# Hash attention and a gated feed-forward: the first batch's preparation rearranged across ScalarE, VectorE, GpSimd and the DMA queues

## The chip, the cores and the metric

The kernel runs on one core of one Trainium2 chip. The metric is the device time of the program in microseconds. A core has TensorE (PE in the profile, with its weight loads as PEld), VectorE (DVE), ScalarE (ACT), GpSimd (POOL) and SyncE (SP, which here only issues DMAs).

## The reference

For 4 batches and 8 heads of 768 tokens by 64, attention is masked by a hash: a query sees the keys that lie in the same of 64 buckets. The result is laid out token by token and goes through an RMS norm and a gated feed-forward.

```python
q_bits = (np.einsum('bhsd,dk->bhsk', q, proj) > 0)          # 6 bits; the same for k
q_bucket = np.sum(q_bits * powers, axis=-1)
mask = q_bucket[:, :, :, None] == k_bucket[:, :, None, :]
scores = np.where(mask, scale * np.matmul(q, k.transpose(0, 1, 3, 2)), -1e9)
attn = softmax(scores)                                       # with + 1e-09 in the divisor
attn_out = np.matmul(attn, v)
x = attn_out.transpose(0, 2, 1, 3).reshape(3072, 512)
xn = x / sqrt(mean(x * x) + 1e-06) * rms_g
out = (silu(xn @ w_gate) * (xn @ w_val)) @ w_out             # 512 -> 1536 -> 512
```

## The kernel before, in words

**The order.** Nothing is scheduled by a planner. Each step is put on one list with a position (`at(pos, fn)`), the list is sorted by position at the end, and the program is issued in that order. Each engine works through its own steps in that order, and so do the DMA queues of SP and of POOL. Position n is the place of slot n; negative positions are the start.

**Units and slots.** A unit is half a batch's queries (384 of 768) for all 8 heads; there are 8 units. A unit has 24 slots: slot n is head n // 3 and a third of its keys. `scores` (L344) makes two matmuls of 71 rows by 384 queries, and ACT takes the exponential of each (L351) into `p`. `pv(n)` follows some slots later: six matmuls that add p times v (L375), and once per pair of heads one with `vsum` (L363). `post` (L391, L392) divides by the sum on DVE. `pvpool` has one buffer, so the next pair's first pv waits for it.

**The 71 rows.** The mask is in the product. A tile `qk` holds 64 rows of q or k, six rows of bits (+0.5 or -0.5) and a constant row; a score whose bits differ falls far below the others, and the exponential drops it. So before a slot can run, its pair of heads must be prepared:
- `tr_mm` (L202): three fp32 transposes of a loaded block on PE; `tr_ev`: its copy to qT or kT by ACT (L209) or DVE (L211). Steps j = 0 and 2 are q of the two heads, 1 and 3 are k.
- the hash: matmuls with the projection. Pairs A and B (batch 0, first two) use `hash_head` per head (L245), C and D (the other two) and later pairs `hash_mm` for the whole pair (L216). Four matmuls stand side by side in four column groups of PE.
- the bits: either `direct_head` or `direct` (L252, L222), in which DVE writes six rows straight into qk, or `bits` (L229), in which DVE writes all groups to a tile and `place` (L235) carries each group of six rows to qk by a DMA of SP.
- `dims_head`, `dims`: the 64 rows of qT or kT cast to fp16 into qk, by POOL (L266, L276), DVE (L264, L274) or ACT (L262). In `dims(c, e)` c = 0 is q, 1 is k, and e is the half (first or second 384 tokens). Unit 0 needs the first half of q and both halves of k; q's second half (0, 1) is for unit 1.
- `vcast` (L280 on DVE and POOL) and `vsum` (L288 to L291, three adds on POOL): v in fp16 and its sums.

**Around them.** PSUM has `ring` (4 buffers: scores, transposes, pair hashes, transposed x), `gvpool` (3: head hashes, some of unit 0's scores, later the gates) and `pvpool`. Loads of q and k (L71, L72) and of v (L78) are issued by SP into four stage buffers each. Weights are loaded by POOL's queue: `load_gv` (L174) gate and value, `load_wo` (L178).

**After a unit.** `queue_norm`: `rstd` (a power on POOL, L443), three `xn` on DVE (L450), transposes on PE (L463), copies to xnT. `queue_gates`: 12 steps, each eight matmuls (L502), a tanh on ACT (L511), two DVE products (L519, L528). For unit 0 the norm stands at position 24.6, its transposes at 30.8, its gates from 32 on, between unit 1's slots; the output matmuls (L566) follow in the next unit. Batch 1's first two pairs are prepared at positions 17.3 (pair (1,0)) and 24.56 (pair (1,1)), with DVE copies in part, and their `dims` at positions 32.2 to 41.5.

Of the kernel before, what the change touches and what calls it, by code (L numbers as in the profile page):

```python
# [22 lines left out]
HQ = 384  # L23
# [10 lines left out]
def kernel(  # L34
# [12 lines left out]
    nc = tc.nc  # L47
# [4 lines left out]
    work = ctx.enter_context(tc.tile_pool(name="work", bufs=2))  # L52
    ring = ctx.enter_context(tc.tile_pool(name="ring", bufs=4, space=PSUM))
# [6 lines left out]
    def at(pos, fn):  # L60
        queue.append((pos, len(queue), fn))
# [5 lines left out]
    def load_qk(b, hp):  # L67
        ql = stage.tile([128, 2, 6, D], FP32, name="ql", tag="ql")
        kl = stage.tile([128, 2, 6, D], FP32, name="kl", tag="kl")
        hs = slice(2 * hp, 2 * hp + 2)  # L70
        nc.sync.dma_start(out=ql, in_=q[b, hs].rearrange("h (p c) d -> p h c d", c=6))  # L71
        nc.sync.dma_start(out=kl, in_=k[b, hs].rearrange("h (p c) d -> p h c d", c=6))  # L72
        loads[(b, hp)] = [ql, kl]

    def load_v(b, hp):
        vl = stage.tile([128, 2, 6, D], FP32, name="vl", tag="vl")
        hs = slice(2 * hp, 2 * hp + 2)
        nc.sync.dma_start(out=vl, in_=v[b, hs].rearrange("h (p c) d -> p h c d", c=6))  # L78
        vloads[(b, hp)] = vl
# [44 lines left out]
    pj1 = []  # L124
# [55 lines left out]

    prep_n = [0]
    qk_of = {}

    def make_prep(b, hp):

# [4 lines left out]
        tl = {}  # L190
# [45 lines left out]
                out=qk[64:70, c, HQ * e : HQ * e + HQ], in_=tl["bits"][base : base + 6, :]  # L236
            )

        GROUPS = [(0, 0), (1, 0), (1, 1), (0, 1)]

        def hash_head(h):
            m = gvpool.tile([128, HQ], FP32, name="hps", tag="gv")
            tl["h", h] = m
            for g, (c, e) in enumerate(GROUPS):
                nc.tensor.matmul(  # L245
# [4 lines left out]
        def direct_head(h, g):  # L250
            c, e = GROUPS[g]
            nc.vector.tensor_scalar(  # L252
                qk[64:70, 2 * c + h, HQ * e : HQ * e + HQ],
                tl["h", h][32 * g : 32 * g + 6, :],
                0.0, 0.5, op0=ALU.is_gt, op1=ALU.subtract,
            )
# [28 lines left out]
        def vsum():  # L285
# [325 lines left out]
    A(-20.5, "tr_mm", 2)  # L611
    A(-20.5, "tr_ev", 2, "a")
    A(-20.4, "tr_mm", 3)
    A(-20.4, "tr_ev", 3, "v")
    A(-20.3, "direct_head", 0, 2)
    at(-20.2, lambda: keep_warm(2))

# [6 lines left out]
    Bp(1.05, "tr_mm", 0)  # L624
    Bp(1.06, "tr_ev", 0, "a")
    Bp(1.1, "tr_mm", 1)
    Bp(1.1, "tr_ev", 1, "v")
    A(1.2, "direct_head", 0, 3)
    A(1.3, "vcast")
    Bp(1.4, "dims_head", 0, 0, 0, "p")  # L630
    Bp(1.4, "dims_head", 0, 1, 0, "p")
# [3 lines left out]
        Bp(2.05, "direct_head", 0, g)  # L635
    Bp(2.1, "tr_mm", 2)
    Bp(2.1, "tr_ev", 2, "a")
    Bp(3.05, "tr_mm", 3)
    Bp(3.05, "tr_ev", 3, "v")
    A(3.1, "direct_head", 1, 3)  # L640
    Bp(3.2, "dims_head", 1, 0, 0, "p")
    Bp(3.2, "dims_head", 1, 1, 0, "p")
    Bp(3.2, "dims_head", 1, 1, 1, "p")
    A(3.3, "vsum")
    Bp(4.05, "hash_head", 1)
    for g in range(3):
        Bp(4.05, "direct_head", 1, g)
    Bp(4.1, "direct_head", 0, 3)
    Bp(4.1, "direct_head", 1, 3)
    Bp(4.5, "vcast")  # L650
    Bp(4.6, "vsum")
    for j in range(4):
        C((4.9, 5.4, 6.0, 6.6)[j], "tr_mm", j)
        C((4.9, 5.4, 6.0, 6.6)[j], "tr_ev", j)
    C(7.6, "hash_mm")
    C(7.6, "direct", 0)
    C(7.6, "direct", 2)
    C(7.6, "bits")
    for i, (c, e) in enumerate(PLACES[2:]):
        C((7.61 if e == 0 or c > 1 else 12.0) + 0.01 * i, "place", c, e)  # L660
    for i, (c, e) in enumerate([(0, 0), (1, 0), (1, 1)]):
        C(7.9 + 0.1 * i, "dims", c, e, "ppv"[i])
    C(8.3, "vcast", nc.vector)
    C(8.5, "vsum")
    for j in range(4):
        Dp(8.1 + 0.8 * j, "tr_mm", j)
        Dp(8.1 + 0.8 * j, "tr_ev", j)
    Dp(11.4, "hash_mm")
    Dp(11.4, "bits")
    for i, (c, e) in enumerate(PLACES):  # L670
        Dp((11.41 if e == 0 or c > 1 else 12.2) + 0.01 * i, "place", c, e)
    for i, (c, e) in enumerate([(0, 0), (1, 0), (1, 1)]):
        Dp(13.7 + 0.3 * i, "dims", c, e, "v")
    Dp(14.8, "vcast", nc.vector)
    Dp(11.5, "vsum")
    for i, P in enumerate((A, Bp, C, Dp)):
        P((15.0, 19.0, 28.5, 31.5)[i], "dims", 0, 1)


    for c in range(4):  # L680
        for wh in range(2):
            at((7.0, 11.8, 14.0, 16.0)[c] + 0.1 * wh, lambda c=c, wh=wh: load_gv(c, wh))
# [52 lines left out]
    for u in range(NU):  # L735
        base = SLOTS * (u + 1)
# [40 lines left out]
```

## Time and profile before

| | us |
|---|---|
| median of 3 runs (lowest, highest) | 365.52 (365.12, 365.79) |
| the profiled execution, whole | 363.95 |
| its span on the core | 362.2 |
| PE, DVE, ACT, POOL busy in the span | 346.8, 243.3, 239.0, 69.1 |
| mean granted clock of PE | 0.994 |

The span runs from the first instruction to the last; the execution's time has 1.75 us around it. Times in the views are us from the span's start, durations of groups are us in total unless a mean in ns is named. PE's busy time includes time in which a started matmul waits for its operand, so a busy PE is not always a PE at its peak. The page cuts the span into 40 slices of 9.05 us; PE's busy tenths are 8976979899 in the first ten and 9 in nearly all others.

### The profile page before, as it was taken

How to read it: one execution, taken by the hardware profiler on the slowest of the kernel's cores; microseconds unless marked ns; L12 is line 12 of the kernel's file. 1: busy time of each engine (PE TensorE's matmuls, PEld its weight loads, DVE VectorE, ACT ScalarE, POOL GpSimd, SP SyncE). 2: the span in 40 equal slices, each digit the busy share in tenths (PEclk: the TensorE clock that was granted, in tenths of full speed). 3: DMA queues.
4: the chain of work that ended last, by engine and by line, in shares of the span. 5: the costliest groups of instructions: out<-in, count | busy, mean ns of one | idle time of the engine just before them, and what ended most of it. 6: DMA issues, size and time to landing. Idle time of an engine off the chain costs nothing.

```text
span 362.2 us, 8037 instructions
## 1 busy us (share of the span) xinstructions
PE 346.8 (96%) x3081; PEld 213.9 (59%) x3081; DVE 243.3 (67%) x494; ACT 239.0 (66%) x544; POOL 69.1 (19%) x108
## 2 busy tenths in 40 slices
PE   8976979899999999999999999999999999999996
PEld 4544645566656656666656666666566656665653
DVE  5887797957855684767757586666847565476771
ACT  3666677676767777776767766776767766873421
POOL 3699172500000003242000001424000000000000
PEclk9999899999999999999999999999999999999999
DMA  7998987300005505220003703420001100200202
GB/s 245 374 265 126 249 151 169 43 3 2 4 3 173 179 3 179 89 90 2 4 3 93 261 2 121 147 93 1 5 3 53 40 2 0 90 2 1 89 0 87
DMA packets 24030, 31.20 MB, mean 86 GB/s; under 512 B 2084, under 2 KB 20920, under 8 KB 23992
## 3 DMA queue, kind: packets, MB, share of 16 engines
q1 hardware_dynamic: 17768, 25.64, 21.0%
q0 software_dynamic: 5824, 4.72, 8.9%
q8 instruction: 24, 0.39, 0.4%
q10 hardware_dynamic: 400, 0.34, 0.3%
q14 instruction: 14, 0.11, 0.1%
HBM read 28.58 MB, written 6.29 MB: 96 GB/s over the span
## 4 chain that ended last, share of the span: by engine, by line
PE 85%; DVE 12%; issue 1%; ACT 1%; POOL 0%; DVEq 0%
PE v_ps L502 17%; PE o_ps L566 16%; PE g_ps L502 16%; PE s_ps L344 15%; PE pv L375 8%; PE trps L202 5%; DVE qk L274 4%; PE hps L216 3%; DVE xn L450 2%; PE xtp L463 1%; PE pv L363 1%; PE hps L245 1%; PE wps L107 1%; DVE a L519 1%; DVE sq L405 1%; DVE bits L229 1%
## 5 line engine op out<-in xcount | busy, mean ns | idle before, releaser
L351 ACT ACTIVATE p<-s_ps 128x384 f16<-128x384 f32 x384 | 163.3, 493 | 62.6 <-PE s_ps L344 62.3
L344 PE MATMUL s_ps<-qk 71*128 71x384 f16 x384 | 95.3, 328 | 5.4 <-DVE qT L211 1.9
L502 PE MATMUL v_ps<-xnT,wv 128*128 128x384 f16 x384 | 78.1, 326 | 2.4 <-DVE a L519 2.4
L519 DVE SCALAR_TENSOR_TENSOR a<-th,g_ps 128x384 f32<-128x384 f32 x96 | 53.1, 553 | 38.7 <-ACT th L511 37.3
L502 PE MATMUL g_ps<-xnT,wg 128*128 128x384 f16 x384 | 78.4, 325 | 0.3 <-ACT xnT L471 0.2
L375 PEld LDWEIGHTS <-p 128*128 128x128 f16 x1152 | 59.8, 98 | 24.9 <-issue 2.5
L566 PE MATMUL o_ps<-wo,ht 128*128 128x512 f16 (+1 forms) x300 | 68.7, 370 | 0.0
L375 PE MATMUL pv<-v,p 128*128 128x65 f16 x1152 | 66.7, 194 | 1.0 <-DVE x L392 0.7
L511 ACT ACTIVATE th<-g_ps 128x384 f32<-128x384 f32 x96 | 47.9, 499 | 17.4 <-PE g_ps L502 15.4
L528 DVE TENSOR_TENSOR ht<-a,v_ps 128x384 f16<-128x384 f32 x96 | 53.1, 553 | 9.2 <-PE s_ps L344 0.5
L502 PEld LDWEIGHTS <-wv 128*128 128x128 f16 x384 | 37.5, 98 | 29.0 <-issue 4.6
L502 PEld LDWEIGHTS <-wg 128*128 128x128 f16 x384 | 35.1, 97 | 22.7 <-issue 2.2
L566 PEld LDWEIGHTS <-ht 128*128 128x128 f16 x300 | 28.2, 97 | 26.5
L443 POOL TENSOR_TENSOR rs<-ms,mhalf 128x3 f32<-128x3 f32 x8 | 6.9, 862 | 191.4 <-DVE ms L439 191.4
L344 PEld LDWEIGHTS <-qk 71*128 71x128 f16 x384 | 28.6, 99 | 16.9 <-issue 7.4
L576 ACT ACTIVATE osb<-o_ps 128x512 f32<-128x512 f32 (+1 forms) x23 | 13.5, 588 | 23.9 <-PE o_ps L566 23.9
L391 DVE RECIPROCAL r<-pv 128x6 f32<-128x6 f32 x32 | 6.2, 193 | 29.4 <-PE pv L375 29.4
L211 DVE TENSOR_SCALAR kT<-trps 128x384 f32<-128x384 f32 x31 | 16.9, 551 | 10.5 <-PE trps L202 10.3
L280 POOL CAST v<-vl 128x768 f16<-128x768 f32 x14 | 12.4, 885 | 59.4 <-DMA vl<-in_v_dram 36.0
L450 DVE SCALAR_TENSOR_TENSOR xn<-x,rs,grow 128x512 f16<-128x512 f32 x24 | 18.9, 844 | 4.7 <-POOL rs L443 4.6
L209 ACT ACTIVATE qT<-trps 128x384 f32<-128x384 f32 x29 | 14.4, 496 | 10.7 <-PE trps L202 10.7
L274 DVE CAST qk<-kT 64x768 f16<-64x768 f32 x27 | 19.6, 727 | 0.3
(66 smaller groups left out, 278.4 us busy)
## 6 DMA issues: line engine op xcount, KB each, us to landing
vl<-in_v_dram SPq DMA_DIRECT2D x16, 384.0 KB
ql<-in_q_dram SPq DMA_DIRECT2D x15, 384.0 KB
kl<-in_k_dram SPq DMA_DIRECT2D x15, 384.0 KB
out_dram<-osb SPq DMA_DIRECT2D x7, 768.0 KB
qk<-bits SPq DMA_DIRECT2D x110, 4.5 KB
wg<-in_moe_w_gate_dram POOLq DMA_DIRECT2D x4, 384.0 KB, 6.7
wv<-in_moe_w_val_dram POOLq DMA_DIRECT2D x4, 384.0 KB, 8.2
wo<-in_moe_w_out_dram POOLq DMA_DIRECT2D x4, 384.0 KB, 5.1
```

Source lines behind the costliest of these rows:

```text
L202: nc.tensor.transpose(m[:, i, :], src[:, i, :], ident)
L211: nc.vector.tensor_scalar_mul(dst, mm, DIM)
L274: nc.vector.tensor_copy(dst, src)
L344: nc.tensor.matmul(s_ps, qk[0:71, 2 + hh, 128 * jt : 128 * jt + 128], qk[0:71, hh, HQ * hf : HQ * hf + HQ], start=True, stop=True,)
L351: nc.scalar.activation(p, s_ps, AF.Exp, scale=SCL)
L375: nc.tensor.matmul(acc[:, t, hh, :], p[:, 128 * t : 128 * t + 128], v16s[b % 2][:, 2 * (jt % 3) + jt // 3, h, :], start=(n % 6 == 0 and i ...
L450: nc.vector.scalar_tensor_tensor(out=tl["xn"][:, t, :], in0=x_of[u][:, t, :], scalar=tl["rs"][:, t : t + 1], in1=grow, op0=ALU.mult, op1=A ...
L502: nc.tensor.matmul(ps, w[:, kt, fs], xnT[:, kt, :], start=(kt == 0), stop=(kt == 3))
L511: nc.scalar.activation(th, tl[f][0], AF.Tanh, scale=0.5)
L519: nc.vector.scalar_tensor_tensor(out=a, in0=th, scalar=1.0, in1=g_ps, op0=ALU.add, op1=ALU.mult)
L528: nc.vector.tensor_mul(ht_of[u][f], a, v_ps)
L566: nc.tensor.matmul(acc, ht_of[u][f][:, 128 * t : 128 * t + 128], wo[:, f, lo:hi], start=(f == 0), stop=(f == 11),)
```

## The change

All of it lies in batch 0's preparation and in the places of loads, casts and weights up to position 38.
- k's copies of step 3 of A, and of steps 1 and 3 of B, are made by ACT instead of DVE.
- `hash_head` makes three groups instead of four. q's second halves of A and B are hashed together by `hash_second_halves` at 8.9 (four groups, one `bits` write), and placed by four DMAs at 12.6, instead of by four `direct_head`.
- A's vsum stands ahead of B's second dims, B's vsum moves from 4.6 to 6.95. B's second k block and hash, and C's and D's transposes and hashes, move 0.45 to 1.2 positions ahead.
- D's first halves of the first head are written directly, so D has six places instead of eight. The places of C's and D's q second halves move from 12 to 15.
- C's and D's vcast and D's dims (0, 0) and (1, 0) go from DVE to POOL; C's vsum moves from 8.5 to 10.8. C's and D's dims (0, 1) move from 28.5 and 31.5 to 31 and 33.
- The four pairs of gate and value weights move from 7.0, 11.8, 14.0, 16.0 to 15.6, 17.0, 20.0, 25.2. Batch 1's loads move later: (1,0) from 1.5 to 7.5, (1,1) from 4.2 to 10.95, v of (1,0) from 2.0 to 10.96, v of (1,1) from 6.0 to 30.2, (1,2) from 12.5 to 22.5, (1,3) from 13.5 to 26.5. The v casts of (1,1), (1,2), (1,3) move from about 27, 31, 34 to 30.5, 34.3, 38.3.

```diff
+    def hash_second_halves(pairs):
+        m = ring.tile([128, HQ], FP32, name="hps", tag="r")
+        heads = [(p, h) for p in pairs for h in range(2)]
+        for g, (p, h) in enumerate(heads):
+            nc.tensor.matmul(
+                m[32 * g : 32 * g + 32, :], pj1[1], tiles_of[p]["q"][:, h, :],
+                start=True, stop=True, tile_position=(0, 32 * g),
+            )
+        bits = work.tile([128, HQ], FP16, name="bits", tag="bits", bufs=4)
+        nc.vector.tensor_scalar(bits, m, 0.0, 0.5, op0=ALU.is_gt, op1=ALU.subtract)
+        return heads, bits
+
+    def place_second_halves(heads, bits):
+        for g, (p, h) in enumerate(heads):
+            nc.sync.dma_start(
+                out=qk_of[p][64:70, h, HQ : 2 * HQ], in_=bits[32 * g : 32 * g + 6, :]
+            )
...
-        GROUPS = [(0, 0), (1, 0), (1, 1), (0, 1)]
+        GROUPS = [(0, 0), (1, 0), (1, 1)]
...
-    A(-20.4, "tr_ev", 3, "v")
+    A(-20.4, "tr_ev", 3, "a")
...
-    Bp(1.1, "tr_ev", 1, "v")
-    A(1.2, "direct_head", 0, 3)
+    Bp(1.1, "tr_ev", 1, "a")
...
-    Bp(3.05, "tr_mm", 3)
-    Bp(3.05, "tr_ev", 3, "v")
-    A(3.1, "direct_head", 1, 3)
+    Bp(2.6, "tr_mm", 3)
+    Bp(2.6, "tr_ev", 3, "a")
+    A(3.15, "vsum")
...
-    A(3.3, "vsum")
-    Bp(4.05, "hash_head", 1)
+    Bp(3.6, "hash_head", 1)
...
-    Bp(4.1, "direct_head", 0, 3)
-    Bp(4.1, "direct_head", 1, 3)
...
-    Bp(4.6, "vsum")
...
-        C((4.9, 5.4, 6.0, 6.6)[j], "tr_mm", j)
+        C((4.2, 4.6, 5.2, 5.6)[j], "tr_mm", j)
...
-    C(7.6, "hash_mm")
+    C(6.4, "hash_mm")
...
-    C(8.3, "vcast", nc.vector)
-    C(8.5, "vsum")
+    Bp(6.95, "vsum")
+    C(8.0, "vcast")
...
-        Dp(8.1 + 0.8 * j, "tr_mm", j)
+        Dp(7.4 + 0.8 * j, "tr_mm", j)
...
-    Dp(11.4, "hash_mm")
-    Dp(11.4, "bits")
-    for i, (c, e) in enumerate(PLACES):
-        Dp((11.41 if e == 0 or c > 1 else 12.2) + 0.01 * i, "place", c, e)
-    for i, (c, e) in enumerate([(0, 0), (1, 0), (1, 1)]):
-        Dp(13.7 + 0.3 * i, "dims", c, e, "v")
-    Dp(14.8, "vcast", nc.vector)
-    Dp(11.5, "vsum")
+    Dp(10.7, "hash_mm")
+    Dp(10.7, "direct", 0)
+    Dp(10.7, "direct", 2)
+    Dp(10.7, "bits")
+    for i, (c, e) in enumerate(PLACES[2:]):
+        Dp((10.71 if e == 0 or c > 1 else 15.2) + 0.01 * i, "place", c, e)
+    C(10.8, "vsum")
+    Dp(11.1, "dims", 0, 0, "p")
+    Dp(11.2, "dims", 1, 0, "p")
+    Dp(11.6, "dims", 1, 1, "v")
+    Dp(11.9, "vcast")
+    Dp(12.0, "vsum")
+    at(8.9, lambda: second.append(hash_second_halves([(0, 0), (0, 1)])))
+    at(12.6, lambda: place_second_halves(*second[0]))
     for i, P in enumerate((A, Bp, C, Dp)):
-        P((15.0, 19.0, 28.5, 31.5)[i], "dims", 0, 1)
+        P((15.0, 19.0, 31.0, 33.0)[i], "dims", 0, 1)
...
-            at((7.0, 11.8, 14.0, 16.0)[c] + 0.1 * wh, lambda c=c, wh=wh: load_gv(c, wh))
+            at((15.6, 17.0, 20.0, 25.2)[c] + 0.1 * wh, lambda c=c, wh=wh: load_gv(c, wh))
...
-    qk_at(1.5, 1, 0)
-    at(2.0, lambda: load_v(1, 0))
-    qk_at(4.2, 1, 1)
-    at(6.0, lambda: load_v(1, 1))
-    qk_at(12.5, 1, 2)
-    qk_at(13.5, 1, 3)
+    qk_at(7.5, 1, 0)
+    at(10.96, lambda: load_v(1, 0))
+    qk_at(10.95, 1, 1)
+    qk_at(22.5, 1, 2)
+    qk_at(26.5, 1, 3)
...
-            vps = [18.7, 26.9, base + 7.0, base + 10.0]
+            vps = [18.7, 30.2, 34.0, 38.0]
```

More of the change, by code (lines that the diff above doesn't have):

```diff
@@ L182 @@
     qk_of = {}
+    tiles_of = {}
+    def hash_second_halves(pairs):
[14 more added lines that the diff above has]
+            )
     def make_prep(b, hp):
@@ L291, in vsum @@
             nc.gpsimd.tensor_add(vsums[b % 2][:, hp, 0, :, 0:64], t1, t3[:, :, 2, :])
+        tiles_of[(b, hp)] = tl
         parts = dict(locals())
@@ L643 @@
     Bp(3.2, "dims_head", 1, 1, 1, "p")
-    A(3.3, "vsum")
-    Bp(4.05, "hash_head", 1)
+    Bp(3.6, "hash_head", 1)
     for g in range(3):
-        Bp(4.05, "direct_head", 1, g)
-    Bp(4.1, "direct_head", 0, 3)
-    Bp(4.1, "direct_head", 1, 3)
+        Bp(3.6, "direct_head", 1, g)
     Bp(4.5, "vcast")
-    Bp(4.6, "vsum")
     for j in range(4):
-        C((4.9, 5.4, 6.0, 6.6)[j], "tr_mm", j)
-        C((4.9, 5.4, 6.0, 6.6)[j], "tr_ev", j)
-    C(7.6, "hash_mm")
-    C(7.6, "direct", 0)
-    C(7.6, "direct", 2)
@@ L658 @@
-    C(7.6, "bits")
+        C((4.2, 4.6, 5.2, 5.6)[j], "tr_mm", j)
+        C((4.2, 4.6, 5.2, 5.6)[j], "tr_ev", j)
+    C(6.4, "hash_mm")
+    C(6.4, "direct", 0)
+    C(6.4, "direct", 2)
+    C(6.4, "bits")
     for i, (c, e) in enumerate(PLACES[2:]):
-        C((7.61 if e == 0 or c > 1 else 12.0) + 0.01 * i, "place", c, e)
+        C((6.41 if e == 0 or c > 1 else 15.0) + 0.01 * i, "place", c, e)
     for i, (c, e) in enumerate([(0, 0), (1, 0), (1, 1)]):
-        C(7.9 + 0.1 * i, "dims", c, e, "ppv"[i])
@@ L663 @@
-    C(8.3, "vcast", nc.vector)
-    C(8.5, "vsum")
+        C(6.7 + 0.1 * i, "dims", c, e, "ppv"[i])
+    Bp(6.95, "vsum")
+    C(8.0, "vcast")
     for j in range(4):
-        Dp(8.1 + 0.8 * j, "tr_mm", j)
-        Dp(8.1 + 0.8 * j, "tr_ev", j)
-    Dp(11.4, "hash_mm")
-    Dp(11.4, "bits")
-    for i, (c, e) in enumerate(PLACES):
-        Dp((11.41 if e == 0 or c > 1 else 12.2) + 0.01 * i, "place", c, e)
-    for i, (c, e) in enumerate([(0, 0), (1, 0), (1, 1)]):
-        Dp(13.7 + 0.3 * i, "dims", c, e, "v")
@@ L674 @@
-    Dp(14.8, "vcast", nc.vector)
-    Dp(11.5, "vsum")
+        Dp(7.4 + 0.8 * j, "tr_mm", j)
+        Dp(7.4 + 0.8 * j, "tr_ev", j)
+    Dp(10.7, "hash_mm")
[10 more added lines that the diff above has]
+    Dp(12.0, "vsum")
@@ L676 @@
+    second = []
+    at(8.9, lambda: second.append(hash_second_halves([(0, 0), (0, 1)])))
+    at(12.6, lambda: place_second_halves(*second[0]))
     for i, P in enumerate((A, Bp, C, Dp)):
-        P((15.0, 19.0, 28.5, 31.5)[i], "dims", 0, 1)
+        P((15.0, 19.0, 31.0, 33.0)[i], "dims", 0, 1)
     for c in range(4):
         for wh in range(2):
-            at((7.0, 11.8, 14.0, 16.0)[c] + 0.1 * wh, lambda c=c, wh=wh: load_gv(c, wh))
+            at((15.6, 17.0, 20.0, 25.2)[c] + 0.1 * wh, lambda c=c, wh=wh: load_gv(c, wh))
@@ L690, in v_at @@
     def v_at(pos, part, b, hp):
-        if (b, hp) not in ((1, 0), (1, 1)):
+        if (b, hp) != (1, 0):
             at(pos, lambda: load_v(b, hp))
```

## The prediction

> **What bounds the kernel now.** The page's first lines come first: PE is busy for 346.8 of 362.2 us, and the busy tenths show that nearly all of the rest lies in the first fifth. So I cut that fifth into stages at unit 0's slots. I call the n-th `scores` of unit 0 slot n; its two matmuls can be counted in the timeline: slot 0 starts at 8.27, slot 12 at 28.18, slot 18 at 33.29, unit 1's first slot (24) at 42.37, and the first gate at 53.41. Windows view, each pair is busy us and instructions:
>
> ```profile
> 8.27:17.74 9.47, 9.41 (x82) 4.91 (x82) 8.13 (x15) 5.85 (x15) 6.49 (x12) 1.00 1.06 374
> 17.74:28.18 10.44, 8.08 (x83) 4.53 (x82) 8.42 (x15) 6.80 (x16) 9.96 (x14) 1.00 1.06 258
> 28.18:33.29 5.11, 3.89 (x59) 2.70 (x56) 4.13 (x6) 4.68 (x12) 4.96 (x8) 1.00 0.57 75
> 33.29:42.37 9.08, 7.18 (x73) 4.96 (x74) 7.67 (x17) 4.55 (x12) 4.12 (x5) 0.81 1.27 225
> 42.37:53.41 11.04, 9.03 (x103) 5.48 (x103) 9.69 (x21) 8.34 (x21) 7.01 (x8) 1.00 0.94 190
> 53.41:71.00 17.59, 15.79 (x146) 9.90 (x144) 15.14 (x25) 12.15 (x29) 6.70 (x9) 1.00 0.58 114
> ```
>
> The order is PE, weight loads, DVE, ACT, POOL, then clock. In unit 0 (rows one to four) DVE is the fullest engine beside PE, and PE's busy time there is stretched by operands that it waits for: 24 slots hold 24 x (0.33 scores + 0.18 pv) = 12.2 us, 16 transposed blocks at 0.33 = 5.3 and six hashes at about 0.85 = 5.1, together 22.6 us in a stretch of 34.1. After 71 PE is full, so what is won before that stays won. Next, DVE's timeline, to see what it is doing:
>
> ```profile
> 11.47 0.56 DVE L211 TENSOR_SCALAR kT<-trps 128x384 f32<-128x384 f32 x1
> ...
> 16.22 2.73 DVE L252 TENSOR_SCALAR qk<-hps 6x384 f16<-6x384 f32 x5 [0.36 <-PE hps L245]
> ...
> 23.34 1.63 DVE L274 CAST qk<-kT 64x768 f16<-64x768 f32 x1
> 25.00 1.24 DVE L280 CAST v<-vl 128x768 f16<-128x768 f32 x1
> ...
> 31.01 2.60 DVE L274 CAST qk<-kT 64x768 f16<-64x768 f32 x2
> 33.63 0.73 DVE L280 CAST v<-vl 128x768 f16<-128x768 f32 x1
> 34.37 1.08 DVE L274 CAST qk<-qT 64x768 f16<-64x768 f32 x1
> 35.56 0.56 DVE L211 TENSOR_SCALAR qT<-trps 128x384 f32<-128x384 f32 x1
> ```
>
> These are the chain's pieces at 16 to 35 us: five direct writes in a row, then casts, several of which take 1.1 to 1.6 us where the same cast takes 0.55 at 53.33. Pair (1,0)'s first copy, at 35.56, stands behind them, and PE's timeline shows who waits for it:
>
> ```profile
> 36.17 0.48 PE L344 MATMUL s_ps<-qk 71*128 71x384 f16 x2 [1.89 <-DVE qT L211]
> ```
>
> The ring buffer of that scores matmul is freed by that copy; D's bits reach their place at the same moment (PEld L344 waits 2.0 for qk<-bits). The clock is then at 0.5 for 3.4 us (row four's 0.81). Where nothing holds ACT, it sets the pace, 0.39 per exponential:
>
> ```profile
> 28.61 4.70 ACT L351 ACTIVATE p<-s_ps 128x384 f16<-128x384 f32 x12 [0.94 <-PE s_ps L344]
> ```
>
> **The change, part by part.** Slots 0 to 11 (now 19.9 us). DVE loses three k copies (3 x 0.56), four direct writes (4 x 0.56) for one 128x384 bits write (0.56), and C's vcast (1.24): 4.6 of 16.6 us busy. ACT gains 3 x 0.49 = 1.5 on 12.65, so it stays under 85%. On the path: hash B1 now needs only ACT copies and stands ahead of slot 4, so it can begin at about 13.75 instead of 14.7 to 15.3, and B's second direct writes end at 16.35, not 17.9 with two more behind. From there DVE: C's first k copy to 16.9; C's second waits for the ring, to 17.85; hash C 0.9 to 18.75; two direct writes and bits 1.7 to 20.45; cast 1.15 (the middle of 0.55 and 1.63) to 21.6; post 0.75 to 22.35; D's k copy, second halves' bits, D's second k copy, 3 x 0.56, to 24.0; hash D 0.9 to 24.9. Slot 12 follows the next slot at 25.5, against 28.18: **-2.7**, between -1.5 (ACT late each time by a copy) and -3.7. A fourth column group saves PE nothing (four fp32 groups run side by side, 0.85 at 8.85), and the second halves' hash adds 0.85 to PE, covered by its 2.4 us idle in row two; without that cover it costs 0.85.
>
> What is queued behind: A's vsum (1.95) now precedes B's second dims on POOL, ready by 16.5, needed at slot 9 (about 22). On POOL (dims 0.84, vcast 0.83, vsum 1.95, one after the other), C's dims end near 19.7, B's vsum 21.7, C's vcast 22.5, C's vsum 24.5, D's two dims 26.2, D's vcast 27, D's vsum 29. D's dims are needed at slot 18, some 4 us later. If POOL's cover were gone, each us late is a us of stall.
>
> Slots 12 to 17 run at ACT's pace now and afterwards: **0**.
>
> Slots 18 to 23 (now 9.08 us). D's three dims and vcast leave this place on DVE (2.60 + 0.73 + a 0.81 at 30.27); two dims and vcast go to POOL. D's direct writes bring the first slot's bits without a DMA, four places instead of six stand ahead. Floors afterwards: ACT 12 x 0.39 = 4.7; PE 6 x 0.51 + 1.3 + 0.85 = 5.2; DVE four copies 2.1, cast 0.8, post 0.75, sumsq 1.75, bits 0.56 = 6.0. I take 6.0: **-3.1**, from -2.0 (a gap and half clock for 3.4 us stay) to -3.8. The clock fell after a stretch (33.54 to 36.96) with PE busy for 1.53 of 3.42 us, and did not after one with 1.88. By ACT's pace PE would be busy for 0.51 of each 0.78, above both.
>
> SP and the loads. SP issues a place in 0.69 (1.37 for two at 28.68), in order, and waits in between for bits (the 22.64 row below). Load (1,0) goes from 14.21 to behind C's four places, about 23.4, needed by transposes at about 30. Loads (1,1) and v(1,0) go behind D's four places, from about 29.5; the second halves' four places come after those, 31 to 33.6. Unit 1 needs the first at slot 24, 25.5 + 5.1 + 6.0 = 36.6. A 1.15 MB load takes 3.1 us at the first row's 374 GB/s and 6.4 at 180, so it lands at 34 to 37: the cover is 0 to 2 us, and I take 0 cost.
>
> ```profile
> 22.64 13.05 SPq L235 DMA_DIRECT2D qk<-bits  x14
> ...
> 44.61 5.66 SPq L235 DMA_DIRECT2D qk<-bits  x4
> ```
>
> Slot 24 to the first gate (now 11.04). The long piece is xn, 4.42 for three where other units take 2.05, because POOL runs a wo issue, a vcast and a vsum beside it. (1,1)'s vcast and vsum leave, gv3's two issues (0.76 each) come; POOL stays occupied, so I take -0.5, and -0.7 for C's last cast, which stood between xn and xnT (50.98) and moves behind. Against it, rs stands behind v(1,0)'s vcast and vsum (2.8) and gv2 (1.55) on POOL: with landing at 34 to 37 it can start at 38.4 to 41.4, and its input is there at 36.6 + 3.15 = 39.75. I take +0.7 of that: **-0.5**, from -1.3 to +1.5.
>
> The gates (53.41 to 71.00). PE loses 1.8 us, most of it here:
>
> ```profile
> 64.48 0.78 POOL L178 DMA_DIRECT2D wo<-in_moe_w_out_dram  x1
> 65.27 0.85 POOL L280 CAST v<-vl 128x768 f16<-128x768 f32 x1
> 66.07 1.00 POOL L288 TENSOR_TENSOR vt<-vl 128x384 f32<-128x384 f32 x1
> ```
>
> A DVE cast beside these takes 2.76 (64.73 to 67.49), and a v_ps matmul then waits 1.35. POOL's run from 61.3 to 68.3 held two pairs' v; it will hold three, (1,1)'s too, some 10 us, and in proportion 2.6 us are lost: **+0.8**, from -0.3 to +1.8.
>
> Sum: -2.7 + 0 - 3.1 - 0.5 + 0.8 = -5.5. The profiled execution took 363.95, its span 362.2 and 1.75 around it; 363.95 - 5.5 = 358.45. The median of the runs, 365.52, lies 1.57 above that execution, so I forecast 365.52 - 5.5 = 360.0.
>
> The Trainium skill bears on this in "SBUF — State Buffer", "Who interferes with whom": GpSimd and a VectorE copy or cast in a two-port mode share one port pair as an exclusive lock, and the later one blocks fully. The trace agrees: 2.76 for a cast of 0.55 at 64.73. It speaks against a move of casts from VectorE to GpSimd, since both then wait; by the middle of the two rows above the sum stays -5.5, and the rule at its worst is the third rival.
>
> **The rivals.** *The jam (slower).* Loads (1,1) and v(1,0), the weights and the second halves' bits now meet on the DMA queues at 29 to 36. Before, loads issued at 35.80 to 38.11 behind four weight loads held SP's places up until 45.3, 47.5 and 49.6 (the 5.66 row: four places), about 10 us after issue. If v(1,0) lands so late, vcast, vsum and gv2 (4.3) put rs beyond its 45.60 of before once the landing is later than 41.3, and unit 1's first slot behind bits that land later still. At 43.5, rs is at 47.8: +2.2, +0.8 in the gates, -0.7 for the cast, 365.52 + 2.3 = 367.8. For it: the row. Against it: load and weights start about together, and the load issued first.
>
> *ACT becomes the bound.* The three copies stand between exponentials in slots 0 to 5; if all lie on the path (1.5) and slots 18 to 23 take another 0.5, the gain is 3.5: 362.0. For it: 4.70 for 12, without a pause. Against: ACT idle for 7 us of row one and two.
>
> *The lock eats it.* POOL is busy for 9.96 of 10.44 us in row two and gets 3.3 us more (two vcasts, two dims). If C's, B's and D's remaining casts each take 2.2 us longer and D's dims come 1.5 late, some 4.5 of 5.5 is gone: 364.5. For it: the casts of 1.4 to 2.8. Against: most DVE work here reads PSUM and kept 0.55 to 0.56 beside a busy POOL (20.93 to 22.62).
>
> **How the numbers follow.** What this measurement can tell from no change is 0.2%, 0.7 us. Forecast 0.57 (357 to 362.5), ACT 0.14, lock 0.12 (half of it within 0.2%), jam 0.17. Faster 0.57 + 0.14 + 0.06 = 0.77, same 0.06, slower 0.17. The range runs from 357.0 to 367.0 and leaves out the jam's upper half and a gain over 8.5, about 0.14.
>
> **What would show it.** Right: slot 12 near 25.5, slot 24 near 36.6, no DVE cast of C's vcast or D's; clock 1.00 throughout; no PE wait on qk<-bits; first gate near 47.6. Wrong: a POOL wait for v(1,0) past 38, an rs after 43, a new PE wait on qk<-bits at unit 1's start, or 70 us of the old trace reached less than 4 us earlier.

## The result, and the profile after

The changed kernel takes 361.47 us (median of 6 runs, 361.30 to 362.91), the kernel before 365.52 (6 runs, 364.25 to 365.79): ratio 0.9906 (95% interval 0.9882 to 0.9930), 4.05 us less, where 5.5 less was forecast. The two profiled executions are only 1.04 us apart (362.91 against 363.95), since one lies above its median and the other below, so stages are compared from slot 0, which starts at 8.27 before and at 10.22 after (the full clock is granted from 6.24 in the one and from 10.27 in the other).

| us after slot 0 | before | forecast | after |
|---|---|---|---|
| slot 12 | 19.91 | 17.2 | 17.29 |
| slot 23 | 33.39 | | 27.88 |
| unit 1's first slot (24) | 34.10 | 28.3 | 32.83 |
| first gate | 45.14 | 39.3 | 43.65 |
| unit 2's first slot | 71.13 | | 68.22 |

The windows view of after is cut at slots 0, 12, 18, 23 and 24, at the first gate, and 16.8 us into the gates. The columns are those of the prediction's view: PE, weight loads, DVE, ACT, POOL, clock, then the mean busy share of the DMA engines and the GB/s they moved.

```profile
10.22:27.51 17.29, 17.13 (x165) 9.42 (x164) 10.87 (x21) 12.54 (x32) 15.01 (x25) 1.00 0.43 146
27.51:32.52 5.01, 3.69 (x58) 2.63 (x55) 3.62 (x7) 4.77 (x13) 4.85 (x8) 1.00 0.41 133
32.52:38.10 5.58, 5.14 (x70) 3.30 (x67) 4.71 (x14) 4.32 (x11) 1.43 (x2) 1.00 1.17 215
38.10:43.05 4.95, 0.86 (x14) 0.51 (x11) 0.53 (x3) 1.31 (x4) 0.20 (x1) 0.79 1.22 258
43.05:53.87 10.82, 10.48 (x100) 7.05 (x100) 7.30 (x20) 7.74 (x19) 8.61 (x12) 0.78 0.98 143
53.87:70.69 16.82, 16.32 (x153) 10.35 (x152) 14.30 (x27) 12.60 (x30) 1.79 (x2) 1.00 1.11 262
```

Up to slot 23 the kernel is 5.5 us ahead. Then comes a stretch of 4.95 us in which no engine is busy for more than 1.31 us while the DMAs move 258 GB/s (fourth row). The timeline says what for; the bracket is the idle time before the row's first instruction, and what ended it:

```profile
35.37 2.09 SPq L200 DMA_DIRECT2D qk<-bits  x3
37.50 11.81 SPq L255 DMA_DIRECT2D qk<-bits  x12
43.05 0.80 PE L365 MATMUL s_ps<-qk 71*128 71x384 f16 x2 [4.08 <-DMA qk<-bits]
42.85 0.83 POOL L300 CAST v<-vl 128x768 f16<-128x768 f32 x1 [8.90 <-DMA vl<-in_v_dram]
47.26 0.89 POOL L464 TENSOR_TENSOR rs<-ms,mhalf 128x3 f32<-128x3 f32 x1
48.18 2.08 DVE L471 SCALAR_TENSOR_TENSOR xn<-x,rs,grow 128x512 f16<-128x512 f32 x3 [0.34 <-POOL rs L464]
```

Unit 1's first scores need the second halves' bits (`place_second_halves`, L200). SP issued those four places from 34.63 to 37.46; the chain that ended last counts 8.39 us from the first issue to the landing:

```profile
34.63 8.39 DMA qk<-bits
43.05 0.80 PE s_ps L365 x2
```

They stood behind loads (1,1) and v(1,0), which SP issued at 31.75 to 34.58, and those behind the weights of POOL's queue:

```profile
30.76 0.95 POOL L174 DMA_DIRECT2D wg<-in_moe_w_gate_dram  x1
31.71 0.75 POOL L174 DMA_DIRECT2D wv<-in_moe_w_val_dram  x1
32.45 0.76 POOL L174 DMA_DIRECT2D wg<-in_moe_w_gate_dram  x1
33.18 0.77 POOL L174 DMA_DIRECT2D wv<-in_moe_w_val_dram  x1
```

Both queues moved data in this time. From 32 to 43 us the DMA view gives nearly as much to POOL's queue (q0, the weights) as to SP's (q1); the columns are packets, MB, and their time as a share of 16 engines' time:

```profile
q0 software_dynamic: 1684, 1.26, 80.7%
q1 hardware_dynamic: 894, 1.21, 34.5%
```

Four weight loads and three loads of 384 KB are 2.75 MB. At the fourth row's 258 GB/s that is 10.7 us, by estimate, and about the time from the first of these issues to the landings.

So v(1,0) is cast only at 42.85, and rs (the result of `rstd`) runs at 47.26. The pause also cost the clock: granted at 0.5 from 40.98 to 47.81 (6.83 us, before 3.41), which is the 0.78 of the first 10.82 us of unit 1. This is the first rival, the jam, inside a kernel that is still faster.

### The profile page after: what moved, and what is told of

Its sections match the earlier page's. It is cut to its first block, busy times and chain, and to the rows that moved or that the text cites. A ratio compares the mean times of both kernels' runs of the same rounds, so it can differ in the third digit from the quotient of the medians.

```text
span 361.1 us, 8041 instructions
## 1 busy us (share of the span) xinstructions
PE 348.0 (96%) x3081; PEld 215.1 (60%) x3081; DVE 231.4 (64%) x486; ACT 239.9 (66%) x547; POOL 69.4 (19%) x112
## 4 chain that ended last, share of the span: by engine, by line
PE 85%; DVE 5%; POOL 3%; DMA 3%; ACT 2%; issue 1%; SPq 0%; ACTq 0%
PE v_ps L523 17%; PE o_ps L587 16%; PE g_ps L523 16%; PE s_ps L365 15%; PE pv L396 8%; PE trps L222 5%; PE hps L236 2%; DMA qk<-bits 2%; DVE qk L294 2%; PE xtp L484 1%; PE pv L384 1%; PE hps L265 1%; ACT p L372 1%; DMA ql<-in_q_dram 1%; POOL qk L296 1%; POOL vt L308 1%
## 5 line engine op out<-in xcount | busy, mean ns | idle before, releaser
L396 PEld LDWEIGHTS <-p 128*128 128x128 f16 x1152 | 60.0, 98 | 25.6 <-issue 4.4
L396 PE MATMUL pv<-v,p 128*128 128x65 f16 x1152 | 66.4, 194 | 1.7 <-POOL vsum L311 1.3
L523 PEld LDWEIGHTS <-wv 128*128 128x128 f16 x384 | 37.5, 98 | 27.5 <-issue 3.0
L597 ACT ACTIVATE osb<-o_ps 128x512 f32<-128x512 f32 (+1 forms) x23 | 13.5, 588 | 23.9 <-PE o_ps L587 23.9
L300 POOL CAST v<-vl 128x768 f16<-128x768 f32 x16 | 13.3, 832 | 76.2 <-DMA vl<-in_v_dram 76.1
L231 DVE TENSOR_SCALAR kT<-trps 128x384 f32<-128x384 f32 x28 | 15.5, 552 | 12.2 <-PE trps L222 12.1
L229 ACT ACTIVATE qT<-trps 128x384 f32<-128x384 f32 x29 | 14.4, 496 | 10.9 <-PE trps L222 10.7
L471 DVE SCALAR_TENSOR_TENSOR xn<-x,rs,grow 128x512 f16<-128x512 f32 x24 | 16.6, 748 | 4.9 <-POOL rs L464 4.9
L413 DVE TENSOR_TENSOR x<-pv,r 128x384 f32<-128x384 f32 x32 | 17.8, 557 | 1.1
```

The costliest lines, as they stand in the source:

```text
L231: nc.vector.tensor_scalar_mul(dst, mm, DIM)
L396: nc.tensor.matmul(acc[:, t, hh, :], p[:, 128 * t : 128 * t + 128], v16s[b % 2][:, 2 * (jt % 3) + jt // 3, h, :], start=(n % 6 == 0 and i ...
L413: nc.vector.tensor_mul(x_of[u].rearrange("p t (h d) -> p t h d", d=64)[:, :, 2 * hp : 2 * hp + 2, :], acc[:, :, :, 0:64], r.to_broadcast([ ...
L471: nc.vector.scalar_tensor_tensor(out=tl["xn"][:, t, :], in0=x_of[u][:, t, :], scalar=tl["rs"][:, t : t + 1], in1=grow, op0=ALU.mult, op1=A ...
L523: nc.tensor.matmul(ps, w[:, kt, fs], xnT[:, kt, :], start=(kt == 0), stop=(kt == 3))
```

## The experiments

Each kernel is told by its edit. The slots are from one profiled execution, in us after slot 0; each ratio is against before in the same series, where before's median is 365.44 to 365.75. "Late" is a position of the changed kernel, "early" one of the kernel before.

| kernel | median | ratio (interval) | slot 12 | slot 23 | slot 24 | first gate | unit 2 |
|---|---|---|---|---|---|---|---|
| loads early | 356.16 | 0.9745 (0.9719 to 0.9771) | 17.26 | 28.23 | 28.93 | 38.02 | 62.59 |
| bits first | 362.85 | 0.9937 (0.9911 to 0.9963) | 17.26 | 27.87 | 28.57 | 45.12 | 69.69 |
| weights behind the norm | 365.44 | 0.9993 (0.9974 to 1.0013) | 17.27 | 27.89 | 28.59 | 37.96 | 71.91 |
| engines alone | 360.85 | 0.9873 (0.9848 to 0.9898) | 17.27 | 31.09 | 31.79 | 42.39 | 68.96 |
| transfers alone | 358.97 | 0.9818 (0.9779 to 0.9857) | 18.63 | 29.91 | 30.61 | 39.64 | 64.21 |
| old engines, clean transfers | 360.59 | 0.9853 (0.9822 to 0.9885) | 18.63 | 33.04 | 33.55 | 42.76 | 67.32 |
| casts back on DVE | 357.23 | 0.9774 (0.9738 to 0.9810) | 17.27 | 29.18 | 29.88 | 38.96 | 63.53 |
| k copies back on DVE | 357.44 | 0.9773 (0.9746 to 0.9799) | 18.73 | 29.68 | 30.38 | 39.47 | 64.04 |
| direct bits instead of the common hash | 355.07 | 0.9712 (0.9685 to 0.9738) | 17.26 | 28.01 | 28.70 | 37.80 | 62.37 |
| one cast behind post | 355.23 | 0.9712 (0.9689 to 0.9736) | 17.27 | 27.83 | 28.53 | 37.62 | 62.20 |
| v of (1,1) early | 355.94 | 0.9731 (0.9709 to 0.9752) | 17.27 | 28.02 | 28.72 | 38.52 | 63.09 |
| D's q copies on DVE | 356.22 | 0.9739 (0.9716 to 0.9763) | 17.73 | 28.51 | 29.21 | 38.30 | 62.87 |

### What made the jam

**Bits first.** Only the four places go ahead of the loads.

```diff
-    at(12.6, lambda: place_second_halves(*second[0]))
+    at(10.9, lambda: place_second_halves(*second[0]))
```

> The changed kernel, but the second halves' four places stand at 10.9, ahead of the loads of (1,1) and v(1,0), instead of at 12.6 behind them. Jam theory (unit 1's first slot waits 4.08 us because its bits are queued behind 1.15 MB of loads that share the engines with weights): the wait for qk<-bits at unit 1's first slot goes, slot 24 comes 28.6 to 29 us after slot 0 instead of 32.8; rs still waits for v(1,0) (vcast 42.85, rs 47.26 in the changed kernel), so the first gate comes only some 2 us earlier: about 359.5. Rival, the norm chain binds alone (v(1,0), gv2, rs): slot 24 moves but the first gate does not, 361.5. Rival, the places are late by themselves (SP's issue or the hash): the wait stays, 361.5.

362.85, where 359.5 was expected: no gain. Slot 24's wait is gone (28.57), but the jam has only moved on. The waits between 27 and 55 us have the loads in the places' stead, rs is at 48.77, and the first gate comes even later than in after (45.12 against 43.65). The first rival was right here: the chain from v(1,0) to rs binds as well.

```profile
PE trps L222 <- DMA ql<-in_q_dram: 1.9, 1, 1.9
PE trps L222 <- DMA kl<-in_k_dram: 1.6, 1, 1.6
POOL v L300 <- DMA vl<-in_v_dram: 12.0, 1, 12.0
```

The order of bits and loads on SP thus decides which of them comes late, not whether one does. The next two kernels change what moves beside them.

**Loads early.** The changed kernel with loads (1,0), (1,1) and v(1,0) at their old positions. The weights stay late.

```diff
-    qk_at(7.5, 1, 0)
-    at(10.96, lambda: load_v(1, 0))
-    qk_at(10.95, 1, 1)
+    qk_at(1.5, 1, 0)
+    at(2.0, lambda: load_v(1, 0))
+    qk_at(4.2, 1, 1)
```

> The changed kernel with the loads of (1,0), (1,1) and v(1,0) at their positions of before (1.5, 4.2, 2.0); weights and everything else as changed. Jam theory: these loads land by about 23 to 25, before any weights move, so the bits find an empty queue and POOL does not wait for v(1,0); no wait for qk<-bits at unit 1's first slot, slot 24 at 28.6 to 29 us after slot 0, rs near 42 to 43 instead of 47.26, first gate 4 to 5 us earlier, of which up to 1.5 is lost in the gates, where v(1,1) lands earlier and its casts on POOL meet DVE's: about 357.5. Rival, loads late are what helps (C's bits were held up by them before): C's or D's slots wait for bits again, 361.5 or more.

356.16: 5.3 us less than the changed kernel, 9.3 less than before. The windows view from slot 18 on (slot 24 at 37.31, the first gate at 46.40) has the clock at 1.00 throughout:

```profile
30.67:37.31 6.64, 5.83 (x78) 3.74 (x75) 5.64 (x14) 5.02 (x13) 5.93 (x8) 1.00 1.23 173
37.31:46.40 9.09, 8.64 (x103) 5.54 (x103) 7.18 (x21) 8.14 (x21) 4.64 (x6) 1.00 1.27 190
46.40:63.22 16.82, 16.32 (x153) 10.35 (x152) 13.79 (x27) 12.60 (x30) 0.85 (x2) 1.00 1.07 248
```

The loads now go out at 14.15 to 18.08, rs is at 40.55, and no wait for bits is left at slot 24. So the moved loads, costed at nothing in the prediction, cost 5.3.

**Weights behind the norm.** The changed kernel's loads stay late; all gate and value weights go behind rs.

```diff
-            at((15.6, 17.0, 20.0, 25.2)[c] + 0.1 * wh, lambda c=c, wh=wh: load_gv(c, wh))
+            at((24.7, 24.8, 24.9, 25.2)[c] + 0.1 * wh, lambda c=c, wh=wh: load_gv(c, wh))
```

> The changed kernel with all four pairs of gate and value weights behind the norm's power on POOL (24.7 to 25.2), so that loads (1,1), v(1,0) and the second halves' bits have the DMA engines to themselves. Theory A, the jam needs the weights: 1.15 MB pass in 3 to 4 us instead of 9, bits land by 39 to 40 (slot 0 at 10.2), the wait at unit 1's first slot falls from 4.08 us to under 1, and what is won is partly lost again to gates that wait for their weights: 358 to 360.5. Theory B, the order on SP's queue alone makes the jam: the wait stays above 2.5 us, 361.5 or more.

Theory A was right about the wait and wrong about the time. Without weights beside them the same late loads do no harm up to the first gate: slot 24 comes at 28.59, v(1,0) is cast at 36.42 (28.06 after slot 0, where after has 32.63), and the first gate is at 37.96.

```profile
36.42 0.83 POOL L300 CAST v<-vl 128x768 f16<-128x768 f32 x1 [7.46 <-DMA vl<-in_v_dram]
```

But the gates then wait for their weights, and a half-clock stretch of 6.83 us follows (56.42 to 63.25): 365.44, which can't be told from before.

```profile
PE v_ps L523 <- DMA wv<-in_moe_w_val_dram: 6.9, 2, 5.7
```

The jam thus needs both, the late loads with their places and the weights issued ahead of them. Early loads undo it, and so do absent weights, but only the early loads bring the time down.

### What each half of the change earns

**Engines alone.** The changed kernel's engines with all loads, weights and v casts where before had them.

```diff
-            at((15.6, 17.0, 20.0, 25.2)[c] + 0.1 * wh, lambda c=c, wh=wh: load_gv(c, wh))
+            at((7.0, 11.8, 14.0, 16.0)[c] + 0.1 * wh, lambda c=c, wh=wh: load_gv(c, wh))
...
-    qk_at(7.5, 1, 0)
+    qk_at(1.5, 1, 0)
...
```

> The changed kernel's work on the engines (k copies on ScalarE, the second halves' hash, direct writes, casts on GpSimd, earlier transposes), with all positions of loads, weights and batch 1's v as before. Theory, the engines' rearrangement earns the 5.5 us between slot 0 and slot 23: slot 23 stays 27.5 to 29.5 us after slot 0 (33.4 before, 27.9 changed), the weights' DMA slows D's places and the second halves' bits by 3 to 5 us each, and POOL's issues come ahead of D's casts: about 360, between 358.5 and 361.5. Rival, the moved transfers earn it: slot 23 goes back to 32 us or more after slot 0, 364 or more.

360.85, 4.6 less than before. The total lies in the expected range, slot 23 does not (31.09 against 27.5 to 29.5). Slot 12 is as early as in after (17.27), but slots 12 to 24 take 14.5 us. POOL's casts of C and D share its queue with weight issues again, and the DVE cast beside them, undisturbed 0.55, takes 2.02:

```profile
26.81 2.02 DVE L294 CAST qk<-kT 64x768 f16<-64x768 f32 x1
```

The next post waits for that cast, a pv matmul for the post (2.2 in this kernel's waits, `PE pv L396 <- DVE x L413`), and the clock falls for 6.83 us at 29.12.

**Transfers alone.** Before's engines with the changed kernel's loads, weights and v casts.

> The kernel before with only the loads of batch 1, the gate and value weights and batch 1's v casts at their changed positions. Theory, the engines' rearrangement earns the time: DVE still delays (1,0)'s copies and slots 18 to 23, slot 23 at 31.5 to 33.5 us after slot 0; v(1,0) lands some 10 us after its issue behind D's places and rs comes later than the 45.60 of before: 365 to 367. Rival, the moved transfers earn it: 362 to 363.

358.97, 6.5 less than before, where next to nothing was expected: the expectation missed. The engines' work is the same as before's and yet slots 12 to 24 take 11.98 instead of 14.19; part of that is the half-clock stretch of before (36.96 to 40.37), which this execution doesn't have. DVE's timeline of this kernel shows the place; before's rows for the same casts are in the prediction (2.60 at 31.01, 0.73 at 33.63):

```profile
28.73 0.54 DVE L274 CAST qk<-qT 64x768 f16<-64x768 f32 x1
29.20 1.50 DVE L274 CAST qk<-kT 64x768 f16<-64x768 f32 x2
30.71 0.56 DVE L280 CAST v<-vl 128x768 f16<-128x768 f32 x1
```

Before slot 12 it is the same: C's cast and vcast take 0.86 and 0.70 instead of 1.63 and 1.24. By the rows of both kernels, POOL, which before issued weights at 21.25 to 22.96, here starts C's dims 1.7 us sooner after slot 0 and is through with them when DVE casts; no run isolates this. At 29.20 POOL does issue weights (27.11 to 30.32), as it did at 31.01 before; why a cast takes 0.75 beside one run of issues and 1.3 beside the other is not settled by any run here.

In this kernel the loads do not jam. D's places stand behind them, so SP issued the loads at 25.53 to 26.94, ahead of the weights, and v(1,0) is cast at 31.17. D's places, issued from 27.14 behind these loads, come late instead, and slot 18 waits for them:

```profile
PE s_ps L344 <- DMA qk<-bits: 2.1, 1, 2.1
```

**Old engines, clean transfers.** Before's engines with the loads of the "loads early" kernel.

> The work on the engines of the kernel before, with the transfers of the early-loads kernel (loads of (1,0), (1,1), v(1,0) as before; weights, v(1,1) and the later loads as changed). Theory A, the weights' move alone frees the engines (POOL's issues no longer meet DVE's casts, the weights' DMA no longer holds D's bits): as the moves-only kernel, slot 23 some 29.5 to 30 us after slot 0, no wait for qk<-bits at slot 18, about 357.5 to 359. Theory B, the engines' rearrangement is still worth most of its 5.5 us on top of clean transfers: slot 23 at 32 us or more, 361 or more. The early-loads kernel, with both, gave 356.2.

360.59: 4.4 behind the new engines on the same transfers. It has the same wait for D's bits at slot 18 (1.89, at 33.66), and in its profile the clock then falls for 6.83 us, so slots 12 to 24 take 14.92. The transfers-alone kernel waited as long there and kept its clock in its profile. So neither theory holds whole: the wait that A ruled out is there, and the time falls just short of B's 361. The two kernels below take back the casts and the copies and cost 1.1 and 1.3 of the 4.4. The likely rest is that D's first bits are now written directly, so that slot 18 has no wait that can take the clock down; no run takes back these direct writes alone, so this is a reading and not shown.

**Casts back on DVE.** From "loads early", C's vcast and D's dims and vcast return to DVE.

```diff
-    C(8.0, "vcast")
+    C(8.3, "vcast", nc.vector)
...
-    Dp(11.1, "dims", 0, 0, "p")
-    Dp(11.2, "dims", 1, 0, "p")
-    Dp(11.6, "dims", 1, 1, "v")
-    Dp(11.9, "vcast")
+    for i, (c, e) in enumerate([(0, 0), (1, 0), (1, 1)]):
+        Dp(13.7 + 0.3 * i, "dims", c, e, "v")
+    Dp(14.8, "vcast", nc.vector)
```

> The early-loads kernel with C's and D's vcast and D's three dims on DVE at their positions of before (8.3, 13.7 to 14.3, 14.8). Theory A, with the weights gone from that stretch the casts cost DVE 0.55 to 0.75 each and lie beside ACT's exponentials: at most 0.7 us slower than 356.2. Theory B, as forecast (casts off DVE are most of the -3.1 of slots 18 to 23): 2 to 3 us slower, 358.5 to 359.

357.23, 1.07 more (intervals 0.9738 to 0.9810 and 0.9719 to 0.9771 overlap); slot 24 is 0.95 later. POOL's casts earn no more than that, and it is no plain cost: slots 12 to 18 take 4.07 instead of 5.03 and slots 18 to 24 take 8.54 instead of 6.64, so the casts cost 1.9 where they stand and half of it is won ahead of them. Three of this kernel's six runs have a mean clock of 0.998 to 1.000 and take 355.85 to 356.22, as "loads early" does; the other three, at 0.990 to 0.994, take 358.23 to 359.04 and carry the difference of the medians.

**k copies back on DVE.** From "loads early", the three `tr_ev` of A and B go back.

```diff
-    A(-20.4, "tr_ev", 3, "a")
+    A(-20.4, "tr_ev", 3, "v")
...
-    Bp(1.1, "tr_ev", 1, "a")
+    Bp(1.1, "tr_ev", 1, "v")
...
-    Bp(2.6, "tr_ev", 3, "a")
+    Bp(2.6, "tr_ev", 3, "v")
```

> The early-loads kernel with the three k copies (A's step 3, B's 1 and 3) on DVE again. Theory, the copies and the earlier hash of B earn part of the -2.7 of slots 0 to 11: slot 12 about 0.8 to 1.5 us later than 17.3 us after slot 0, 357 to 357.7. Rival, ACT sets the pace, so copies on DVE cost nothing: 356.2 or less.

357.44, 1.28 more; slot 12 goes from 17.26 to 18.73, and nothing is made up later: unit 2's first slot is 1.45 later. The intervals overlap, but the traces place the loss, so the three copies on ACT are worth 1.3 to 1.5.

**Direct bits instead of the common hash.** From "loads early", `hash_head` makes four groups again and four `direct_head` write the second halves' bits.

```diff
-        GROUPS = [(0, 0), (1, 0), (1, 1)]
+        GROUPS = [(0, 0), (1, 0), (1, 1), (0, 1)]
...
+    A(1.2, "direct_head", 0, 3)
...
+    A(3.1, "direct_head", 1, 3)
...
+    Bp(4.1, "direct_head", 0, 3)
+    Bp(4.1, "direct_head", 1, 3)
...
-    at(8.9, lambda: second.append(hash_second_halves([(0, 0), (0, 1)])))
-    at(12.6, lambda: place_second_halves(*second[0]))
```

> The early-loads kernel with A's and B's second halves' bits written by four direct writes at their positions of before, and no common hash or places for them. Theory, three DVE writes more (1.7 us) lie on the path of slots 0 to 11 and one hash less on PE (0.85) gives part back: 0.5 to 1.5 us slower, 356.7 to 357.7. Rival, that hash costs PE more than DVE wins: 355.5 to 356.

355.07, the lowest median: 10.4 us less than before, 6.4 less than after, 1.1 less than "loads early" (the intervals 0.9685 to 0.9738 and 0.9719 to 0.9771 just overlap). Slot 12 stays at 17.26, so the four DVE writes that the common hash saves were not on the path. Whether the hash's own 0.85 on PE and its four places on SP cost anything is not shown: unit 2's first slot is only 0.22 earlier than in "loads early".

### What the fastest version leaves

**One cast behind post.** From the fastest, D's k cast (1, 1) moves from 11.6 to 13.7, behind the post that waits for it.

```diff
-    Dp(11.6, "dims", 1, 1, "v")
+    Dp(13.7, "dims", 1, 1, "v")
```

> The direct-heads kernel (355.1) with D's last dims cast on DVE at 13.7, behind the post of the second pair, instead of at 11.6 ahead of it. Theory, that cast meets D's vcast and vsum on POOL (1.17 us instead of 0.55) and holds up the post, and so the first pv of the third pair, by about 1.2 us: 0.3 to 1.2 us faster, 354 to 354.8. Rival, ACT sets the pace there (its gap is 0.25 us) and nothing moves: 355.1.

355.23 against 355.07: nothing. Slots 12 to 23 gain 0.2; DVE's order there doesn't set the pace.

**D's q copies on DVE**, on top of it.

```diff
-        Dp(7.4 + 0.8 * j, "tr_ev", j)
+        Dp(7.4 + 0.8 * j, "tr_ev", j, "v")
```

> The cast-behind-post kernel with D's two q copies on DVE too. Theory, ACT sets the pace of slots 7 to 23 and is freed of two copies (0.78 us): 0.3 to 0.8 us faster than that kernel. Rival, DVE's queue (direct writes, post) delays the copies, the ring and so D's hash: 0 to 0.8 slower.

356.22, 1.0 more (the intervals overlap): slot 12 is at 17.73, 0.46 later, and unit 2's first slot 0.67 later. Taking copies from ACT doesn't help either; as with the k copies, a copy costs more on DVE than on ACT.

**v of (1,1) early.** From the fastest, its load goes back to 6.0 and the v casts of (1,1), (1,2), (1,3) to their old positions.

```diff
+    at(6.0, lambda: load_v(1, 1))
...
-            vps = [18.7, 30.2, 34.0, 38.0]
+            vps = [18.7, 26.9, base + 7.0, base + 10.0]
```

> The direct-heads kernel (355.1) with v of (1,1) loaded at 6.0 and the v casts of (1,1), (1,2), (1,3) at their positions of before. Theory, those casts and sums on POOL then meet xn and DVE's casts in the gates again: xn takes up to 4.4 us instead of 2.1 and the gates lose 1 to 2 us (first gate to unit 2's first slot 25.5 to 26.6 us instead of 24.6): 356 to 357.5. Rival, with the loads clean their place does not matter: 355.1.

355.94, 0.87 more (the intervals overlap); in the traces 0.72 of it lies ahead of the gates. The three xn take 3.61, without the edit 2.08, and the first gate is 0.72 later. The gates cost the same 24.57 as without it.

```profile
41.49 3.61 DVE L471 SCALAR_TENSOR_TENSOR xn<-x,rs,grow 128x512 f16<-128x512 f32 x3
41.42 0.79 POOL L174 DMA_DIRECT2D wg<-in_moe_w_gate_dram  x1
42.22 0.75 POOL L174 DMA_DIRECT2D wv<-in_moe_w_val_dram  x1
42.95 0.76 POOL L178 DMA_DIRECT2D wo<-in_moe_w_out_dram  x1
43.69 0.86 POOL L300 CAST v<-vl 128x768 f16<-128x768 f32 x1
62.86 0.83 POOL L300 CAST v<-vl 128x768 f16<-128x768 f32 x1 [14.34 <-DMA vl<-in_v_dram]
```

## Why the prediction was right, and where it was wrong

**The total.** 361.47 lies between forecast (360.0) and no change, inside the range; the sign and the size came out. That it came so near is luck. The jam took 5.3 us that the sum had at nothing, and without it ("loads early") the kernel gains 9.3 us, far more than the 5.5 that the sum promised. The stages below add up to -2.9 at unit 2's first slot and not to -4.05, since they are read from two executions that are 1.04 us apart where the medians are 4.05 apart.

**Slots 0 to 11: -2.7 forecast, -2.6 measured.** Slot 12 is at 17.29 against 17.2. What carries it is the copies on ACT: undone, 1.47 of it goes in the trace. The other 1.2 to 1.3 is what the transfers-alone kernel gains too (18.63), so the two ways are not additive: the engines alone reach 17.27 with the weights still early. The saved direct writes, counted among DVE's 4.6 us, bring slot 12 nothing ("direct bits", 17.26 with and without them).

**Slots 12 to 17: 0 forecast, -0.1 measured** (5.01 against 5.11).

**Slots 18 to 24: -3.1 forecast, +1.45 measured** (32.52 to 43.05 is 10.53, before 9.08). Without the jam the term comes near the forecast: slots 18 to 24 take 6.64 with the loads early (-2.4), against 6.0 predicted. The attribution was at best half right. The prediction gave the gain to casts leaving DVE. Casts back on DVE cost 1.9 in these slots, but about 1 up to slot 24, and with no cast moved at all the transfers alone take 2.2 from slots 12 to 24, the missing half clock included. The prediction's own rows had casts of 0.8 to 1.6 us that take 0.55 elsewhere; it charged them to DVE instead of asking what stood beside them.

**SP and the loads: 0 forecast, 5.3 measured. This is the step that failed.** The prediction took a load of 1.15 MB to last 3.1 to 6.4 us from its issue, by its first row's 374 GB/s and by 180 GB/s, which none of its rows shows, and so to land at 34 to 37. The places issued from 34.63 landed 8.39 later, and v(1,0), issued at 34.02, was cast at 42.85. Two things were missing from the working. POOL's four weight loads of 384 KB each were issued from 30.76, before the loads at 31.75, while the prediction argued against its own rival that "the load issued first"; 2.75 MB and not 1.15 MB stood ahead of the bits. And the wait was costed as a landing alone, with nothing for the clock, which here fell to 0.5 for 6.83 us. All four signs that the prediction named as wrong are there: a wait for v(1,0) past 38, rs after 43, a wait for qk<-bits at unit 1's start, and less than 4 us gained at 70 us of the old trace (2.9 from slot 0 to unit 2's first slot). The rival itself put the landing of v(1,0) at 43.5 on before's time scale and its deciding point at 41.3. With slot 0 1.95 later, the cast at 42.85 stands at 40.90 on that scale, rs at 45.31 (before 45.60) and unit 1's first slot at 41.10 (before 42.37): the jam came, and v(1,0) landed 0.4 us short of the point from which rs would have come later than before. That a wrong step left a right sign is luck, too.

**Slot 24 to the first gate: -0.5 forecast, -0.2 measured**, with half clock for the first 4.76 us of it. With the loads early, so with neither half clock nor a late rs, it is 9.09, or -1.95. The three xn fell from 4.42 to 2.08, which -0.5 had assumed would not happen ("POOL stays occupied"): weight issues stand beside them (48.12 to 51.89) and do them no harm here; the vcast and vsum of (1,1), which stood beside them before, have left.

**The gates: +0.8 forecast, -1.4 measured** (first gate to unit 2's first slot 24.57, before 25.99). The sign was wrong. The step assumed that (1,1)'s v would join a run of POOL work beside DVE's casts. It was loaded so late that POOL waited 17.01 us and cast it at 68.90, when only the last of DVE's casts in this stretch, at 69.04, was left. In the engines-alone kernel, with loads, weights and v casts at their old places, POOL starts on v at 59.29, a DVE cast beside it takes 2.75 and the stretch 26.57. The old places of the v casts are not enough for that: in "v of (1,1) early" the gates take 24.57 again. There POOL waits 14.34 us for the next v and casts it at 62.86, just after DVE's last cast began (62.29). So it is the landing of v that keeps the two apart, by luck, and which of the moved transfers delays it stays open.

**The three xn.** What "v of (1,1) early" loses is lost in xn. Of the three, 0.75, 1.31 and 1.71 us long, the last stands beside (1,1)'s vcast (43.69 to 44.55); the second has only weight issues beside it, and why it is slow there and not in after (0.74) stays open.

**The other rivals.** *ACT as the bound* did not come where it was put: ACT is busy for 12.54 of the first 17.29 us, and taking copies off it costs time (D's q copies, k copies). *The lock* did not eat the gain: the Trainium skill's rule in "SBUF — State Buffer", "Who interferes with whom", that GpSimd and a VectorE copy or cast in a two-port mode lock each other out, spoke against moving casts to POOL. The moved casts ran in 0.82 to 0.84 on POOL and the kernel gained at most about 1 us by them, so here the rule costs less than the move brings; for the 2.02 cast of the engines-alone kernel the trace agrees with it.

**What the two halves are worth together.** Engines alone -4.6, transfers alone -6.5, both as changed -4.05, both with early loads -9.3. The change held more than it showed: on the new engines the later weights, with the later v of (1,1) and last two pairs, bring 4.7 (360.85 to 356.16), and the later loads of (1,0), (1,1) and v(1,0) undid 5.3.

## What to carry to other kernels

When a transfer is moved later, list everything that is issued ahead of it on every queue, not only on its own, and take its landing time from a row with the same company; and if PE waits for it, add what a lower clock would cost. When a cast or a copy takes two or three times its undisturbed row, look first for what runs beside it: here casts of 1.63 and 1.24 us took 0.86 and 0.70 on the same engine once the transfers had moved. Then run the two halves of a mixed change apart, since the best version was neither half nor the whole.

## What the hardware showed that was not expected

**The clock's price comes in steps.** The transfers-alone kernel's six runs differ by 4.3 us and fall into three pairs by the mean granted clock: 356.74 and 357.05 at 1.000, 358.70 and 359.24 at 0.995, 361.04 and 360.26 at 0.990 and 0.989. One stretch of 3.41 us at half clock is 0.005 of such a span, so each pair seems to have one stretch more than the last, at about 1.9 us each. The same wait of about 2 us at slot 18 would then bring none, one or two; only the first execution has a trace, so where the others lost their clock is not shown. The price is not the same everywhere: for before, executions at 0.993 to 0.995 and at 0.990 to 0.991 are about 1 us apart, and for the engines-alone kernel those at 0.995 (360.46, 360.95) are no faster than those at 0.990 and 0.991 (360.29 to 361.65). The Trainium skill, "TensorE: Matmul & The Clock Gate", Part 1, gives windows of 3413 ns, which agrees with the 3.41, and an idle window as what halves the clock; before's clock fell after a window in which PE was busy for 1.53 of 3.42 us, so it was not an idle one.

**A place's time to land depends on its company.** The four places of 4.5 KB each were waited for until 8.39 us after the first issue where loads and weights stood ahead of them; with the loads early, issued from 29.77, no matmul waited for them.
